# Merging the weights' sign into the exponent word on VectorE, with the prologue loads in one written list

## The chip, the cores and the metric

The kernel runs on one core of a Trainium2 chip. The metric is device time in microseconds (us) of one execution. Of the kernel before the change there are three timed runs: 801.87, 797.59 and 800.38 us, median 800.38 us. Every engine of the core has an instruction queue of its own, which it works through in order: TensorE (PE in the profile; its weight loads are PEld), VectorE (DVE), ScalarE (ACT), GpSimd (POOL) and SyncE (SP, which here only issues DMAs).

## The reference

Two stages. The first is a recurrence over 768 steps in 32 independent heads (batch 4, 8 heads of width 40). Its output is reshaped to 3072 tokens of width 320 and goes through a small network:

```python
for t in range(S):                       # state: (B, H, 40, 40)
    y[:, :, t] = einsum('bhd,bhde->bhe', rt, state)
    Sa = einsum('bhde,bhe->bhd', state, at)
    state = state * wt[:, :, None, :] - einsum('bhd,bhe->bhde', Sa, bt) + einsum('bhd,bhe->bhde', vt, kt)
h = x @ w_in                             # x: (3072, 320), w_in: (320, 2048)
out = (h * cos(h)) @ w_out               # w_out: (2048, 320)
```

The weights w_in and w_out arrive as float64, that is as pairs of 32-bit words, and the kernel turns them into float32 itself.

## The kernel before the change

The recurrence is cut into 24 chunks of 32 steps. For each chunk the kernel forms small triangular matrices and inverts them, and then carries the state on with a fixed series of steps: `ch_t` (transpose of the state), `ch_q`, `ch_x`, `ch_s` and `ch_z`, which leaves the new state in `qz` and the chunk's output in `yt`. In `ch_z` VectorE adds into `qz` (L755) and `yt` (L762), then GpSimd scales `qz` (L756) and `yt` (L767), and `tokens` sends `yt` through memory (`xd`) into the layout `xT` that the second stage reads. The loads of a chunk's k, v and r feed GpSimd's `p2_in` (copies to `vp` and `rp`, L586) and `p2_kn` (L593, L594). The network is worked on for two chunks at a time in pieces of four blocks of w_in and w_out (`first_a`, `first_b`, `second`); from chunk 2 on these pieces are dealt out between the recurrence's steps.

**The weights.** w_in and w_out are turned into float32 in 20 pieces of 128x512 (`rounded`), in this order of instructions per piece n:

- `fetch` (token `wf`): SP loads the words into a buffer that five pieces in turn share (from piece 7 on three).
- `taken` (`wt`): VectorE takes the mantissa bits (L245) and the exponent bits (L246) of the high word; ScalarE makes the float32 exponent (L249, Relu) and, in the kernel before, the sign of the high word as bf16 (L251).
- `mantissa` (`wm`): VectorE adds the low word to the mantissa (L255), ScalarE scales it (L258).
- `product` (`wp`): VectorE multiplies mantissa and exponent (L261); in the kernel before GpSimd then multiplies the result by the sign in place (L264).

The pieces are staggered. In program order one slot is `wm n`, `wt n+1`, `wp n`, then the fetch that takes over the buffer of piece n, and then the next slot. The slots lie between the recurrence's steps of chunks 0 to 3, from 48 to 140 us of the span. A fetch waits until the buffer's last reader is done, and everything behind it on SP's queue waits too.

**Idle matmuls.** In the same stage PE is given matmuls on zeros, whose results nobody reads: `busy` (128x512) and `spare` (128x192), in fixed numbers between the steps.

**What sets the order.** Inside `manual_schedule` each engine takes its instructions in the order in which they are written. In the kernel before that order comes out of a program of counters: `step` (L346) runs one step and then what is due after it (`later`, L343, so many steps later), and deals out the waiting parts of the weights and of the inverse. Instructions outside of `manual_schedule` (constants, the first loads of L182 to L201, and `warm`, L204, a Sin on one element that is there to load ScalarE's function table) are put into the queues by the framework's own scheduler.

Of the kernel before, what the change touches and what calls it, by code (L numbers as in the profile page):

```python
# [14 lines left out]


# [4 lines left out]
def kernel(  # L21
# [49 lines left out]
    NF = DFF // P  # L71
    N72 = C + D
# [109 lines left out]
    for c in range(2):  # L182
        load(c, "w", parts=range(2))
        load(c, "w", nc.scalar, range(2, 4))
    load(0, "a")
    load(1, "a", nc.scalar)
    for n, c in (("w", 2), ("w", 3), ("a", 2), ("a", 3), ("b", 2)):
        load(c, n)
    ws_fetch(1)
    load(3, "b")  # L190

# [8 lines left out]
    for c in range(2):  # L200
        load(c, "b", nc.gpsimd)  # L201
# [22 lines left out]
    def rounded(m, dst, src, by, by_sb):  # L224
# [3 lines left out]
        pool, tag = (  # L228
            ((sb2, "gT"), (sb2, "gT"), (sb1, "nt"), (sb1, "u"), (sb1, "inv"))[m % 5]
            if m < 10 else ((sb1, "nt"), (sb1, "u"), (sb1, "inv"))[(m - 10) % 3]  # L230
        )
# [9 lines left out]
        def taken():  # L241
            hi = t["words"][:, :, 1]
            t["mant"] = sb2.tile([P, WID], I32, tag="mant", name="mant")
            t["expo"] = sb2.tile([P, WID], I32, tag="expo", name="expo")
            nc.vector.tensor_scalar(t["mant"], hi, 0xFFFFF, None, ALU.bitwise_and)  # L245
            nc.vector.tensor_scalar(  # L246
                t["expo"], hi, 20, 0x7FF, ALU.logical_shift_right, ALU.bitwise_and
            )
            nc.scalar.activation(t["expo"], t["expo"], ACTF.Relu, bias=to_bits, scale=2.0**23)  # L249
            t["sign"] = sb2.tile([P, WID], mybir.dt.bfloat16, tag="sign", name="sign")  # L250
            nc.scalar.activation(t["sign"], hi, ACTF.Sign)  # L251
# [8 lines left out]
        def product():  # L260
            nc.vector.tensor_tensor(  # L261
                dst, t["mant"].bitcast(F32), t["expo"].bitcast(F32), ALU.mult
            )
            nc.gpsimd.tensor_tensor(dst, dst, t["sign"], ALU.mult)  # L264

        return fetch, taken, mantissa, product

    def weights():
# [5 lines left out]
        def put(dst, src, by, by_sb):  # L274
# [9 lines left out]
            work.append((fetch, none, none, lambda: nc.scalar.mul(dst, dst, by)))  # L284
# [52 lines left out]
    G = {"rest": []}  # L337

    waiting = []

    inv_steps, w_steps = [], []

    def later(steps, work):  # L343
        waiting.append([steps, work])

    def step(work, of_inv=0, of_w=0, small=False):  # L346


        before = list(waiting)
        work()  # L350
        G["small"] = small and G["kind"]
        for w in before:
            w[0] -= 1
            if w[0] == 0:
                waiting.remove(w)
                w[1]()
        for steps, n in ((inv_steps, of_inv), (w_steps, of_w)):
            for _ in range(min(n, len(steps))):
                steps.pop(0)()


    def p1_w(c):
# [21 lines left out]
        if c == 8:  # L384
            later(2, lambda: over_w(c, unpad(nat["w", c])))
        elif c >= 4:
            over_w(c, unpad(nat["w", c]))
# [18 lines left out]
    def p1_a(c):  # L406
        if c >= 4:
# [5 lines left out]
            over_w(c + 1, unpad(nat["w", c + 1]))  # L413
# [13 lines left out]
    def p1_b(c):  # L427
# [7 lines left out]
        if c == 2:  # L435
            G.pop("lower")()

    def p1_n(c):
# [15 lines left out]
        if c % 4 == 0:  # L454
            G["nt"] = sb1.tile([P, C, 4, 2, HH], F32, tag="nt", name="nt")
            if c < 8:
                G["noff"] = sb2.tile([P, 4, 2, HH, C], F32, tag="rt", name="noff")
        for e in range(2):
            nc.scalar.copy(
                G["nt"][:, :, c % 4 : c % 4 + 2, e, :].rearrange("p t c j -> p c j t"),  # L460
# [3 lines left out]
        def lower():  # L464
            for e in range(2):
                nc.scalar.copy(
                    G["noff"][:, c % 4 : c % 4 + 2, e, :, :].rearrange("p c j t -> p c (j t)"),
# [3 lines left out]
        if c == 0:  # L471
            G["lower"] = lower
        elif c < 8:
            lower()
        if c % 4 == 2 and c > 2:
            inv_space()

    def inv_space():
        G["inv"] = sb1.tile([P, C * C], F32, tag="inv", name="inv")
        nc.gpsimd.memset(G["inv"], 0.0)  # L480
        nc.gpsimd.memset(G["inv"][:, :: C + 1], -1.0)

    def inv_start():

        G["u"] = sb1.tile([P, C, C], F32, tag="u", name="u")
        nc.vector.transpose(
            G["u"].rearrange("p t s -> p (t s)"), G["nt"].rearrange("p t c e j -> p (t c e j)")
        )

    def inv_step(j):  # L490
        u, x = G["u"], G["inv"].rearrange("p (t s) -> p t s", t=C)
# [8 lines left out]
    def inv_end(c, part=False):  # L500
        rt = sb2.tile([P, 4, H, C], F32, tag="rt", name="rt")
        nc.vector.transpose(
            rt.rearrange("p c h t -> p t (c h)"), G["inv"].rearrange("p (t s) -> p t s", t=C)
        )
        G["rts"] = rt
# [8 lines left out]
    def pair_step(j):  # L514
        u, x = G["u"], G["inv"]
# [11 lines left out]
    def pair_turn(c):  # L527
        if c:
            G["rn"] = sb1.tile([P, 4 * H, HB], F32, tag="nt", name="rn")
            G["half"] = sb1.tile([P, 4 * H, C], F32, tag="u", name="half")  # L530
            nc.gpsimd.memset(G["half"][:, :, HB:], 0.0)
        else:
            G["rn"] = bn_b[6].rearrange("p h d -> p (h d)").rearrange("p (n u) -> p n u", u=HB)
        nc.vector.transpose(
            G["rn"].rearrange("p n u -> p u n"), pick(G["inv"], 0, (1, HB), (C, C)),
# [7 lines left out]
    def pair_half(c, i):  # L543
        return G["half"][:, H * i : H * (i + 1)] if c else bn_b[4 + i % 2][:, :, :C]

    def pair_first(c, i, moe=True):
        ps = pair_space(c, moe, ps_h, "h")
        nt = G["noff"].rearrange("p c e j t -> p (c e j) t")
        half = pair_half(c, i)
        for n in range(H):  # L550
            for g in range(B):
                mm(
                    ps[blk[g], HB * n : HB * (n + 1)], nt[blk[g], H * i + n, :],
                    G["rn"][blk[g], H * i + n, :], n == 0,
# [5 lines left out]
    def pair_second(c, i, moe=True):  # L560
        ps = pair_space(c, moe, ps_o, "o")
        half, rt = pair_half(c, i), G["rts"][:, i]
# [9 lines left out]
    def by_blocks(c):  # L572
        return [
            inv_start, *(lambda j=j: pair_step(j) for j in range(HB - 1, 0, -1)),
            lambda: pair_turn(c), lambda: inv_end(c, True),
        ]

    def inverse(c):
        return [
            inv_start, *(lambda j=j: inv_step(j) for j in range(C - 1, 0, -1)), lambda: inv_end(c)  # L580
        ]


    def p2_in(c):
        for dst, m in ((vp, "v"), (rp, "r")):
            nc.gpsimd.tensor_copy(  # L586
# [3 lines left out]
        landed(c)  # L590

    def p2_kn(c):
        nc.gpsimd.tensor_tensor(unpad(kn_b[c % 2]), nat["k", c], G["rw", c], ALU.mult)  # L593
        nc.gpsimd.tensor_copy(vvm[c % 2][:, :, C : C + D], nat["v", c])  # L594
        landed(c)

    def landed(c):

        G["users", c] = G.get(("users", c), 0) + 1
        if G["users", c] == 2 and c + 1 < NCH:  # L600
            for i, n in enumerate("kvr"):
                later(3 + i if c > 1 else 1, lambda n=n: load(c + 1, n))

    def p2_v(c):
# [3 lines left out]
        G["vT"] = sb3.tile([P, 4, P], F32, tag="opT", name="vT")  # L608
        G["rT", c] = sb2.tile([P, 4, P], F32, tag="rT", name="rT")
        nc.scalar.copy(G["vT"].rearrange("p j t -> p (j t)"), ps[:, 0])  # L610
        nc.scalar.copy(G["rT", c].rearrange("p j t -> p (j t)"), ps[:, 1])

    def p2_k(c):
        ps = at("kT")
        turned(ps[:, 0], kn_b[c % 2])
        G["kT"] = sb3.tile([P, 4, P], F32, tag="opT", name="kT")
        nc.scalar.copy(G["kT"].rearrange("p j t -> p (j t)"), ps[:, 0])

    def p2_g(c):
        kT, vT, aT, rT = G["kT"], G["vT"], G["aT", c], G["rT", c]  # L620
# [29 lines left out]
    def ch_t(c):  # L650
        ps = at("sT")
        n = DP + D
        G["s"] = sb1.tile([P, 2 * B, n], F32, tag="s", name="s")
# [4 lines left out]
        for i in range(2):  # L658
            nc.scalar.copy(G["s"][:n, 4 * i : 4 * i + 4].rearrange("p i e -> p (i e)"), ps[:n, i, : 4 * n])  # L659

    def ch_q(c):
        ps = at("qps")
        for i in range(2 * B):
            for e in range(2):
                for f in range(2):
                    mm(
                        ps[half[e], f, i * C : (i + 1) * C], G["s"][half[f], i, half[e]],
# [8 lines left out]
    def ch_x(c):  # L676
# [21 lines left out]
        G["x0"] = x0  # L698

    def ch_s(c):  # L700
        ps = at("sps")
        x0 = G["x0"]
# [21 lines left out]
        G["sm"] = sm  # L724

    def ch_z(c):
        ps = [at("dps") for _ in range(2)]
        sm = G["sm"]
# [41 lines left out]
        later(2, lambda: tokens(c, yt))  # L770

    def tokens(c, yt):

        xd = dram.tile([DM, P], F32, tag="xd", name="xd")
# [5 lines left out]
        if c % 2 == 0:  # L780
            G["xT"] = sb2.tile([P, 3, 2 * P], F32, tag="xT", name="xT")
        xT, toks = G["xT"], slice((c % 2) * P, (c % 2 + 1) * P)
        G["xT", c // 2] = xT
# [6 lines left out]
        later(1, back)  # L790


    def first_a(g, j):
        rest(3)
        G["ph"] = [ps_h.tile([P, 512], F32, tag="h", name="ph").rearrange("p (f t) -> p f t", f=2)
                   for _ in range(2)]
        G["gT", j] = sb2.tile([P, 4, 2 * P], F32, tag="gT", name="gT")
        first_full(g, j, 0)

    def first_full(g, j, e, fresh=True):  # L800
        xT, ph = G["xT", g], G["ph"][e]
# [5 lines left out]
    def first_b(g, j):  # L807
        xT, phs = G["xT", g], G["ph"]

        def tails(fresh):  # L810
            for f in range(2):
                for e in range(2):
                    for to in (full if G["small"] == "q" else [every]):
# [12 lines left out]

        us = [ph.rearrange("p f t -> p (f t)") for ph in phs]
        ns = [sb2.tile([P, 4 * P], F32, tag="turns", name="turns") for _ in range(2)]
        for u, n in zip(us, ns):
            nc.scalar.activation(n, u, ACTF.Identity, bias=rnd, scale=1.0)  # L830
        for u, n in zip(us, ns):
            nc.vector.scalar_tensor_tensor(n, n, -ROUND, u, ALU.add, ALU.subtract)  # L832
        gT = G["gT", j]

        def cosine(n):
            nc.scalar.activation(n, n, ACTF.Abs)  # L836
            nc.scalar.activation(n, n, ACTF.Sin, bias=half_pi, scale=-2.0 * math.pi)  # L837

        def product(e):
            nc.vector.tensor_tensor(  # L840
                gT[:, 2 * e : 2 * e + 2].rearrange("p f t -> p (f t)"), us[e], ns[e], ALU.mult
# [331 lines left out]
```

## Time and profile before

| | |
|---|---|
| timed runs | 801.87, 797.59, 800.38 us (median 800.38) |
| profiled execution, span from first to last instruction | 798.9 us |
| PE busy | 745.9 us (93%) |
| DVE busy | 486.7 us (61%) |
| ACT busy | 383.4 us (48%) |
| POOL busy | 199.9 us (25%) |
| L251, ScalarE's sign | 20 instructions, 13.3 us |
| L264, GpSimd's sign product | 20 instructions, 26.6 us |

The span of the profiled execution is the only time that is known of it; it lies inside the range of the three timed runs. The first 100 us differ from the rest: PE is not full there (17.10 us busy of 20 from 60 to 80 us, 15.65 from 80 to 100), and its granted clock is 0.82 to 0.92 in the 20 us slices up to 100 us and 1.00 in all later ones. From 320 us on PE is busy for 79.67 of 80 us and 390.00 of 398. The profile's lists name the source line, the engine, the operation and the tiles written and read; a start time is counted from the span's start, and "idle before" tells how long the engine had nothing to run and what ended that.

### The profile page before, as it was taken

What the parts mean: (1) busy time and instruction counts of PE and PEld (TensorE: products, weight loads), DVE (VectorE), ACT (ScalarE), POOL (GpSimd) and SP (SyncE); (2) the same over time, 40 slices, a digit from 0 to 9 for tenths busy, and PEclk for the clock granted to TensorE, in tenths of its full rate; (3) what the DMA queues carried; (4) which work ended last, traced back from release to release, by engine and by line L of the source; (5) the groups of instructions that cost most, each with busy time, mean ns of one, the idle gap of its engine ahead of it and who ended that gap; (6) DMA issues with size and microseconds to landing.
All of it is one profiled execution on the core that took longest, in us unless ns stands there. A gap on an engine that the chain in (4) does not pass through costs nothing.

```text
span 798.9 us, 39602 instructions
## 1 busy us (share of the span) xinstructions
PE 745.9 (93%) x17812; PEld 571.0 (71%) x17812; DVE 486.7 (61%) x1025; ACT 383.4 (48%) x723; POOL 199.9 (25%) x354
## 2 busy tenths in 40 slices
PE   4768798999999999999999999999999999999997
PEld 4535576777766777777777787777787777777775
DVE  8768858864734896554895645994346863323331
ACT  1336567564435436545535635534545445354352
POOL 5326635230321330330330230332031122201000
PEclk9888899999999999999999999999999999999999
DMA  8575563343353314334214324223220222001000
GB/s 112 150 187 140 146 152 88 60 124 64 59 122 64 67 36 65 72 99 70 60 38 66 93 43 73 46 49 68 43 46 21 46 46 55 19 18 32 20 17 16
DMA packets 183304, 55.79 MB, mean 70 GB/s; under 512 B 157152, under 2 KB 178656, under 8 KB 183136
## 3 DMA queue, kind: packets, MB, share of 16 engines
q1 hardware_dynamic: 177440, 52.11, 30.6%
q8 instruction: 140, 2.29, 1.2%
q10 hardware_dynamic: 5440, 0.82, 0.8%
q0 software_dynamic: 256, 0.33, 0.3%
q14 instruction: 28, 0.23, 0.1%
HBM read 42.07 MB, written 11.14 MB: 67 GB/s over the span
## 4 chain that ended last, share of the span: by engine, by line
PE 65%; DVE 14%; DMA 5%; ACT 5%; issue 4%; POOL 3%; SPq 2%; DVEq 0%; ACTq 0%; POOLq 0%
PE ph L101 22%; PE po L101 20%; PE x0ps L101 3%; PE dps L101 3%; PE gram L101 3%; DVE rw L395 3%; PE vT L330 2%; PE sps L101 2%; PE qps L101 2%; PE nps L101 2%; DVE inv_tmp L494 2%; DVE inv L498 2%; DVE mant L245 1%; SPq L152 1%; PE kT L330 1%
## 5 line engine op out<-in xcount | busy, mean ns | idle before, releaser
L101 PE MATMUL po<-w_out_sb,gT 128*128 128x320 f32 x768 | 223.5, 439 | 0.1
L101 PE MATMUL ph<-xT,w_in_sb 128*128 128x256 f32 x768 | 185.7, 386 | 0.1
L101 PEld LDWEIGHTS po<-w_out_sb,gT 128*128 128x128 f32 x768 | 140.2, 190 | 54.6 <-issue 2.3
L101 PEld LDWEIGHTS ph<-xT,w_in_sb 128*128 128x128 f32 x768 | 139.3, 190 | 29.7 <-issue 12.4
L830 ACT ACTIVATE turns<-ph,rnd 128x512 f32<-128x512 f32 x96 | 64.1, 685 | 156.3 <-PE ph L101 155.9
L832 DVE SCALAR_TENSOR_TENSOR turns<-turns,ph 128x512 f32<-128x512 f32 x96 | 64.0, 683 | 109.4 <-ACT turns L830 109.2
L840 DVE TENSOR_TENSOR gT<-ph,turns 128x512 f32<-128x512 f32 x96 | 65.8, 686 | 38.4 <-ACT turns L837 38.4
L756 POOL TENSOR_TENSOR qz<-qz,wc 128x160 f32<-128x160 f32 x92 | 41.9, 475 | 168.5 <-DVE qz L755 167.9
L837 ACT ACTIVATE turns<-turns,half_pi 128x512 f32<-128x512 f32 x96 | 69.3, 722 | 3.1
L836 ACT ACTIVATE turns<-turns 128x512 f32<-128x512 f32 x96 | 60.1, 626 | 19.0 <-DVE turns L832 19.0
L101 PE MATMUL ph<-xT,w_in_tail 64*128 64x256 f32 (+1 forms) x512 | 54.6, 394 | 1.6 <-issue 1.6
L498 DVE TENSOR_TENSOR inv<-inv,inv_tmp 128x31 f32<-128x31 f32 (+15 forms) x124 | 51.2, 413 | 4.3
L755 DVE TENSOR_TENSOR qz<-dps,qz 128x160 f32<-128x160 f32 x92 | 28.9, 314 | 37.6 <-PE dps L101 37.3
L586 POOL COPY vp<-nat_v 128x320 f32<-128x320 f32 x24 | 11.7, 487 | 159.9 <-DMA nat_v<-in_v_dram 139.6
L494 DVE TENSOR_TENSOR inv_tmp<-u,inv 128x31 f32<-128x31 f32 (+15 forms) x124 | 48.5, 391 | 2.3
L395 DVE RECIPROCAL rw<-nat_w 128x320 f32<-128x320 f32 x20 | 42.8, 2142 | 0.1
L101 PEld LDWEIGHTS ph<-xT,w_in_tail 64*128 64x128 f32 (+1 forms) x512 | 32.2, 160 | 10.8 <-issue 7.3
L767 POOL TENSOR_TENSOR yt<-yt,wb 128x512 f32<-128x512 f32 x24 | 31.6, 1318 | 22.1 <-DVE yt L762 22.1
L659 ACT COPY s<-sT 104x416 f32<-104x416 f32 x46 | 20.8, 503 | 33.1 <-PE sT L655 33.1
L719 DVE TENSOR_TENSOR sm<-sps,su 128x128 f32<-128x128 f32 x48 | 11.7, 285 | 33.1 <-ACT sm L714 30.3
L396 POOL TENSOR_TENSOR bn<-nat_b,rw 128x320 f32<-128x320 f32 x22 | 19.9, 905 | 44.3 <-DVE rw L395 44.2
L671 ACT COPY qz<-qps 40x512 f32<-40x512 f32 x46 | 26.6, 579 | 6.8 <-PE qps L101 6.4
(136 smaller groups left out, 1100.3 us busy)
## 6 DMA issues: line engine op xcount, KB each, us to landing
words<-in_moe_w_in_dram SPq DMA_DIRECT2D x8, 512.0 KB
xd<-yt SPq DMA_DIRECT2D x48, 80.0 KB
out_dram<-ot SPq DMA_DIRECT2D x24, 160.0 KB
nat_k<-in_k_dram SPq DMA_DIRECT2D x92, 40.0 KB
nat_v<-in_v_dram SPq DMA_DIRECT2D x92, 40.0 KB
nat_r<-in_r_dram SPq DMA_DIRECT2D x92, 40.0 KB
nat_a<-in_a_dram SPq DMA_DIRECT2D x84, 40.0 KB
ws<-in_w_dram SPq DMA_DIRECT2D x5, 640.0 KB
```

Source lines behind the costliest of these rows:

```text
L101: nc.tensor.matmul(o, lhsT=lhsT, rhs=rhs, start=start, stop=stop, skip_group_check=True)
L395: nc.vector.reciprocal(rw, wn)
L494: nc.vector.tensor_tensor(tmp, u[:, j : j + 1, :j].to_broadcast([P, C - j, j]), x[:, j:, j : j + 1].to_broadcast([P, C - j, j]), ALU.mult,)
L498: nc.vector.tensor_tensor(x[:, j:, :j], x[:, j:, :j], tmp, ALU.subtract)
L755: nc.vector.tensor_tensor(z, pick(dp, 0, (2 * N72 + C, 2), (N72, 2), (1, D)), z, ALU.add)
L756: nc.gpsimd.tensor_tensor(z, z, wc.rearrange("p (f m b) -> p f m b", f=2, m=2)[:, :, :, bb] .unsqueeze(3).to_broadcast([P, 2, 2, D]), ALU. ...
L767: nc.gpsimd.tensor_tensor(yt.rearrange("p j b t -> p (j b) t"), yt.rearrange("p j b t -> p (j b) t"), wx, ALU.mult)
L830: nc.scalar.activation(n, u, ACTF.Identity, bias=rnd, scale=1.0)
L832: nc.vector.scalar_tensor_tensor(n, n, -ROUND, u, ALU.add, ALU.subtract)
L836: nc.scalar.activation(n, n, ACTF.Abs)
L837: nc.scalar.activation(n, n, ACTF.Sin, bias=half_pi, scale=-2.0 * math.pi)
L840: nc.vector.tensor_tensor(gT[:, 2 * e : 2 * e + 2].rearrange("p f t -> p (f t)"), us[e], ns[e], ALU.mult)
```

## The change

**The sign.** ScalarE's Sign (L251) and GpSimd's product (L264) are gone. A new step `signed` (token `wg`), one VectorE scalar_tensor_tensor, takes the sign bit of the high word and merges it by bitwise or into the exponent word that ScalarE has made. It stands right ahead of `wp n`, so a slot becomes `wm n`, `wt n+1`, `wg n`, `wp n`, fetch. Since it reads the words once more, the buffer of piece n comes free after `wg n` and no longer after `wm n`.

```diff
             nc.scalar.activation(t["expo"], t["expo"], ACTF.Relu, bias=to_bits, scale=2.0**23)
-            t["sign"] = sb2.tile([P, WID], mybir.dt.bfloat16, tag="sign", name="sign")
-            nc.scalar.activation(t["sign"], hi, ACTF.Sign)
+
+        def signed():
+            nc.vector.scalar_tensor_tensor(
+                t["expo"], t["words"][:, :, 1], -(2**31), t["expo"], ALU.bitwise_and, ALU.bitwise_or
+            )
...
             nc.vector.tensor_tensor(
                 dst, t["mant"].bitcast(F32), t["expo"].bitcast(F32), ALU.mult
             )
-            nc.gpsimd.tensor_tensor(dst, dst, t["sign"], ALU.mult)
-
-        return fetch, taken, mantissa, product
+
+        return fetch, taken, mantissa, product, signed
```

**The written list.** The counters (`step`, `later`, `piece` and the rest of the control program) are replaced by a list of some 1,200 tokens, `PLAN`, which is read from left to right; each token calls one function (`do`). Its first part:

```python
L:0:w:s:l L:0:w:a:r L:1:w:s:l L:1:w:a:r L:0:a:s:x L:1:a:a:x L:0:b:p:x L:1:b:p:x pw:0 L:2:w:s:x L:3:w:s:x
L:2:a:s:x la:0:vr pa:0 L:3:a:s:x L:2:b:s:x sf:1 L:3:b:s:x wf:0 pw:2 la:0:k wf:1 pa:2 pb:0 pn:0 pb:2 lo:0 pn:2
...
B:5 ip:0:2 ip:0:1 k:1 B:2 it:0 ih:0 g:1 B:3 F:0:0:0 wt:0 wt:1 wf:3 wf:4 S:0:0:0 wm:0 wg:0 wp:0 s:0 wf:5 wm:1
wt:2 wg:1 wp:1 B:6 z:0 in:2 wf:6 wm:2 B:4 t:1 sf:2 kn:2 ld:4:a wt:3 wg:2 wp:2 wf:7 wm:3 B:3 F:0:1:0 tk:0 v:2
ld:4:w tb:0 wt:4 wg:3 wp:3 wf:8 wm:4 B:4 q:1 ld:3:k wt:5 wg:4 wp:4 wf:9 wm:5 B:5 k:2 ld:5:w ld:3:v wt:6 wg:5
wp:5 wm:6 wt:7 B:4 S:0:1:0 ld:3:r K:6 x:1 wg:6 wp:6 wm:7 wt:8 wg:7 wp:7 B:3 g:2 wf:10 wm:8 wt:9 wg:8 wp:8 B:3
s:1 in:3 wf:11 wm:9 wt:10 wg:9 wp:9 B:6 K:14 z:1 wf:12 wm:10 wt:11 wg:10 wp:10 B:4 K:6 t:2 kn:3 wf:13 wm:11
```

(`L` is one of the first loads with its chunk, tensor and queue, s for SP, a for ACT and p for POOL; `ld`, `la` and `sf` are other loads; `B` and `K` the idle matmuls; `in` and `kn` the GpSimd steps of a chunk; `tk` and `tb` the two halves of `tokens`.) Read out step by step, the counters of the kernel before give the same list, but for three things: the `wg` tokens; the first loads, which stood outside of `manual_schedule` and now stand in it, with the loads of a and b for chunks 2 and 3 written between the first steps; and one step without work that stood behind `fa:10:2`, so that in that piece `first_b` now starts with its wide matmuls and not with its narrow ones.

```diff
-    for c in range(2):
-        load(c, "w", parts=range(2))
-        load(c, "w", nc.scalar, range(2, 4))
-    load(0, "a")
-    load(1, "a", nc.scalar)
-    for n, c in (("w", 2), ("w", 3), ("a", 2), ("a", 3), ("b", 2)):
-        load(c, n)
-    ws_fetch(1)
-    load(3, "b")
...
     su = kept("su", [P, HH, C], 1, 1.0)[0]
...
-    for c in range(2):
-        load(c, "b", nc.gpsimd)
     half_pi = kept("half_pi", [P, 1], 1, math.pi / 2)[0]
     warm = kept("warm", [P, 1])[0]
     nc.scalar.activation(warm, half_pi, ACTF.Sin)
```

On SP the loads keep their order. On POOL the eight loads of b for chunks 0 and 1 now come behind the constants' memsets, where they came between `su` and `half_pi`. On ACT `warm` waits for `half_pi` alone, as before, which is now ready without those eight loads ahead of it. The buffers' rotation is the same (`WORDS`), the idle matmuls write to the newest output tile (`spare`) and not always to the first, and `product` of the network names its operands in two dimensions instead of one.

## The prediction

> **What bounds the kernel now.** I read the busy time by stretches first, then the chain of waits that ended last, then each engine in order of time from 47 to 145 us, the only stretch in which the two lines of the sign run.
>
> ```profile
> 60.00:80.00 20.00, 17.10 (x542) 10.39 (x530) 18.06 (x30) 13.67 (x24) 12.66 (x13) 0.87 0.55 139
> 80.00:100.00 20.00, 15.65 (x393) 10.28 (x392) 18.00 (x34) 12.10 (x23) 13.08 (x15) 0.87 0.55 146
> 100.00:120.00 20.00, 19.92 (x602) 15.81 (x601) 11.70 (x25) 13.33 (x25) 6.65 (x7) 1.00 0.67 153
> ```
>
> The columns behind the length are PE, PEld, DVE, ACT and POOL busy, the granted clock, and DMA. From 60 to 100 us VectorE is the full engine (36.06 of 40 us) and PE is not, although it is given idle matmuls; from 100 us on PE is. So the change can move the end through two doors: VectorE's queue between 62 and 91 us, and afterwards whatever PE waits for. The chain of waits says the same; it runs through the weights' own instructions:
>
> ```profile
> 80.43 0.60 DVE mant L255
> 81.03 1.30 DVE mant L245
> ...
> 86.75 0.64 ACT sign L251
> 87.40 0.38 ACT sm L714 x2
> 87.79 0.49 DVE sm L719 x2
> ...
> 90.70 0.87 POOL w_out_sb L264
> 91.81 0.61 POOL qz L756 x2
> ```
>
> Start, duration, what. Both removed lines stand on it: ScalarE's sign holds up the recurrence's `sm`, and GpSimd's sign product holds up the new state `qz`. PE sees it here:
>
> ```profile
> 88.43 0.32 PE L101 MATMUL dps<-idle 32*64 32x288 bf16 x4 [3.30 <-DVE sm L719]
> ```
>
> **The added instruction.** The nearest row is L255, the same kind on the same words: 20 times, 622 to 1352 ns, median 682, and 0.60 us from one start to the next (72.52, 73.12). Bounds: 0.34 us, the step from L246 to L245 (48.55, 48.89), one source; 1.35 us, L255 at 65.92 beside GpSimd's L593. I take 0.60, since it has L255's two sources: 20 x 0.60 = 12.0 us of VectorE.
>
> **What the removed product gives VectorE.**
>
> ```profile
> 80.58 1.47 POOL L264 TENSOR_TENSOR w_in_sb<-w_in_sb,sign 128x512 f32<-128x512 f32 x1 [3.50 <-DVE w_in_sb L261]
> 80.95 1.38 DVE L245 TENSOR_SCALAR mant<-words 128x512 int32<-128x512 int32 x1
> 85.27 0.42 DVE L245 TENSOR_SCALAR mant<-words 128x512 int32<-128x512 int32 x1
> ```
>
> Beside L264 L245 takes 1.38 us, alone 0.42: 0.96 us lost. In VectorE's order of time this happens beside L264 at 67.78 (L246), 70.29, 73.12, 75.97, 80.95 and 132.95 (0.96 each), 96.77 (0.83), 129.67 (L255, 0.59), 101.13 (0.23) and 119.36 (0.10): 7.5 us. So VectorE's work grows by 12.0 - 7.5 = 4.5 us. The Trainium skill (SBUF — State Buffer, section SBUF: two separate sides) says why: VectorE and GpSimd share one pair of ports, which whoever starts first holds for a whole instruction. It also speaks against the change, because an instruction of VectorE with two sources in SBUF is held by a GpSimd instruction that reads SBUF, and the added one is such; by it the slots beside what is left on GpSimd (L756, L767, L593) would pay again. The trace agrees with both, by the rows above and by the 1.35 us of L255.
>
> **47 to 62 us: nothing.** `wg 0` and `wg 1` fall into waits of VectorE: 1.24 us ahead of L261 at 52.27 (for ScalarE's L258) and 3.89 us before 60.45 (for PE). Without these covers it would be 1.2 us.
>
> **62 to 91 us: -3.3 us, before SP.** Between the two `ch_z` lie `wg 2` to `wg 9`, 8 x 0.60 = 4.8 us, and five of the delays, 5 x 0.96 = 4.8 us: VectorE's work stays level. What goes are its waits for ScalarE, 1.49 us ahead of L697, 0.73 ahead of L643 and 0.89 ahead of L719. Each is behind an exponent that came late because L245 was late, and behind a sign (78.41, 83.39, 86.75; 0.55 us each to the next start). I set the slots again one after the other: slot 2 keeps its delays beside L756 to L594, the next take 2.48 us (0.60 + 0.34 + 0.34 + 0.60 + 0.60) for 2.85. Then `wp 5` ends at 74.1 (before 75.37), L697 starts at 76.65 (79.38), `wp 7` ends at 80.7 (83.19) and `sm` starts at 84.45 (87.79), 3.3 us earlier. PE could take no more than 3.86: its idle matmuls end at 84.25, then it waited 0.56 and 3.30 us.
>
> **A wait that is added on SP.** `wf 7` was free after `wm 2` (issued at 63.21); now it waits for `wg 2`, behind both instructions of `wt 3` (63.07 to 65.06), until 65.7. Behind it on SP are `xd`, `nat_w`, `xT`, two more fetches and the loads of k, v and r of chunk 3, all nearly without a gap to 84.6. `xd` waited until 64.30 anyway, so they move by 1.9 us. Their reader is L586 at 88.08 (v) and 88.47 (r), which stands ahead of `qz` on POOL. r's last load was issued at 84.2; the chain has 2.21 us for the landing of such a load (k, at 15.26), so r was there at 86.4 and will be at 88.3, copied (0.45) by 88.7. `qz` starts then, against 91.81: -3.1 us, which is what the stage yields. This wait is what is late next; the 0.73 us that L264 held up `qz` (91.08 to 91.81) is inside this number. The fetches later on wait for their `wg` less than SP is behind.
>
> **91 to 145 us: +0.3 us.** `wg 10` to `wg 13` fall beside VectorE's 2.86 us wait at 106.42. In 107 to 121 us the sign's 0.55 us on ScalarE and the 0.60 us of `wg` nearly cancel, but `wg 15` stands ahead of L567, for which PE waited 0.72 us at 121.06: up to +0.6. In 122 to 140 us three `wg` cost 1.8 and give back 0.59 + 0.96; ScalarE's copies for PE (0.45 us wait at 133.82, 0.67 at 137.06) come up to 0.55 earlier: -0.6 to +0.3. **After 145 us** nothing has changed and PE is full, so the shift stays.
>
> **The prologue: -0.2 us.** On POOL the eight loads of b, 4.77 us from 2.74, move behind 2.4 us of memsets; they land at 11.2 now and are read by L396 at 12.83 and 15.43, so 2.4 us are nearly covered. `warm` comes earlier on ACT and with it the one table load that is needed, so that of 1.28 us at 6.40 goes; VectorE works without a gap from 8.04 to 15.9, but the chain does not pass there: L396 at 26.68 waits for b of chunk 3 (issued at 21.74, 4.78 us), at the end of SP's row of loads, 3 us after VectorE was ready. SP's order is the same. Bounds: -0.5 (a's loads without b's beside them) and +2 (ACT's loads of w held behind `warm` until 2.8 us instead of 0.81).
>
> **The rest.** `product` in two dimensions: L401 with sixteen short rows takes 669 ns, L840 686, so nothing. The other order of one `first_b`: under 0.2 us. The idle matmuls' other tile: no wait.
>
> **Sum.** -0.2 + 0 - 3.1 + 0.3 = -3.0 us. The profiled span of 798.9 becomes 795.9. The runs' median, 800.38, is 1.5 us above that span, so I predict 797.4 us. One thing I can't price well is PE's clock. After a wait the idle matmuls run slowly, 1.46 us for three at 90.64 against 0.81 at 94.43. If the 3.30 us wait goes, up to 1.6 us more is gained; if PE instead waits for `qz` at 89 us, as much is lost a little later. By the Trainium skill (TensorE: Matmul & The Clock Gate, section Part 1: The HAM clock gate) the clock is either half or full, decided over windows of about 3.4 us; the rows at 90.64 and 94.43 fit that, but do not tell where the window falls.
>
> **Rivals.**
> 1. *More is gained: 794.1 us.* The wait at 88.43 and the slow clock after it both go, r of chunk 3 isn't late because waits between the loads (one of v's issues takes 1.55 us) take up SP's 1.9 us, and ScalarE's relief counts at 133.82 and 137.06: -3.0 - 1.6 - 1.2 - 0.5 = -6.3. For it: POOL and ACT have gaps all through the stage. Against: PE is full from 100 to 120 us.
> 2. *Hidden anyway: 800 us.* PE's idle matmuls have fixed numbers; if they or PE's waits for "issue" (1.54 us at 78.50, 1.57 at 124.11) pace the stage, nothing is gained. Against: the 3.30 us wait.
> 3. *SP is late: 801.4 us.* Should the fetches fall further behind, `in 3` holds `qz` back. It turns to a loss once r lands more than 5.0 us later than 86.4 (86.4 + 5.0 + 0.45 is 91.8); at 6 us it costs 1.0 us.
> 4. *VectorE becomes the bound, slower: 804.9 us.* The place is the slots between `ch_z` 0 and 2. If ScalarE's waits are refilled, and GpSimd's remaining work blocks the new instruction as it blocked L255, VectorE's 4.5 us more count in full. It decides from the point at which VectorE has no idle time left; it has 3.94 us of 40 from 60 to 100 us. For it: that is little. Against: these waits are for ScalarE, which loses 13.3 us of work.
> 5. *The change doesn't do what it says:* the loads in the prologue come into another order (their numbered semaphores are handed out in turn), and ACT's queue stands still behind a large load: +2 to +5 on 797.4, 799 to 802.
>
> **How the numbers follow.** Chances: forecast 0.47 (795 to 799), rival 1 0.20, rival 2 0.11, rival 3 0.05, rival 4 0.10, rival 5 0.07. The bound of 0.5% is 4.0 us (796.4 and 804.4), about what a measurement of this kernel can tell from no change, as its three runs spread over 4.3 us. Faster: rival 1 and a third of the forecast, 0.36. Slower: rival 4 and a little of 3 and 5, 0.12. Same: 0.52. The range takes in the middles of all rivals and all bounds above: 792.5 to 805.0.
>
> **What would show it.** After the change L245 at 0.42 us in nearly all slots; L697 of chunk 1 before 77.5 us and PE's wait for `sm` under 1 us; `qz` of chunk 1 at about 88.7 us, right behind `rp`; `wf 7` at 65.7 us; L396's last load landing near 26.5 us; from 145 us on the same intervals. The prediction is wrong if VectorE shows long rows of L255's kind beside POOL, if `qz` starts after 91 us, or if the first 47 us are longer by more than 1 us.

## The result

The changed kernel is slower. In nine runs each, the kernel before took 797.59 to 803.40 us (median 800.42) and the changed kernel 801.69 to 809.74 us (median 806.44). The recorded ratio is 1.0059, with a 95% interval of 1.0034 to 1.0083; the two medians alone would give 1.0075. The median lies above the forecast's range (792.5 to 805.0). The profiled execution of the changed kernel is one of its shorter ones, 802.93 us with a span of 801.2 us; against the 798.9 us of before it shows 2.3 us of the loss, not all of it. VectorE's busy time went from 486.7 to 491.7 us, GpSimd's from 199.9 to 174.5, ScalarE's from 383.4 to 370.8.

Line numbers after the change: L318 and L319 are `taken` (before L245, L246), L325 is the new instruction, L331 the mantissa, L337 the product, L747 `sm`, L783 and L790 the additions into `qz` and `yt`, L615 `rt`, L310 the fetch of words on SP, L805 `xd`. First the busy time by stretches:

```profile
60.00:80.00 20.00, 14.94 (x539) 9.31 (x518) 18.31 (x36) 10.76 (x19) 6.73 (x9) 0.95 0.59 150
80.00:100.00 20.00, 16.98 (x399) 11.20 (x393) 16.85 (x37) 8.39 (x17) 7.27 (x9) 0.79 0.52 145
100.00:120.00 20.00, 19.53 (x600) 15.18 (x598) 12.79 (x25) 11.48 (x21) 1.16 (x3) 1.00 0.54 133
```

The columns are the stretch and its length, PE, PEld, DVE, ACT and POOL busy, the granted clock, the DMA share and GB/s. GpSimd is relieved (14.00 us from 60 to 100 instead of 25.74), and yet VectorE is as busy as before (35.16 us instead of 36.06). The chain of waits between 84 and 104 us tells what holds it:

```profile
85.17 4.13 DMA words<-in_moe_w_in_dram
...
89.39 0.43 DVE mant L318
...
91.47 0.32 DVE qz L783
...
95.88 1.29 DVE expo L325
...
97.19 0.33 SPq L310
...
98.04 0.37 SPq L805
...
98.45 2.88 DMA xd<-yt
```

The sign of ScalarE, `sm` and GpSimd's product, which stood on it before, are gone. In their place stand the words of piece 10, which SP could fetch only at 85.17, then the new instruction, then SP's queue behind it (fetch 13, and `xd` of chunk 1 behind that fetch). PE shows both sides:

```profile
86.31 0.76 PE L184 MATMUL dps<-idle 32*64 32x288 bf16 x8
...
91.97 0.59 PE L184 MATMUL busy<-idle 128*128 128x512 bf16 x1 [2.82 <-issue]
```

The wait of 3.30 us for `sm` went, as forecast (no bracket in the first line). But PE then had 2.82 us in which it waited for nothing that the profile shows, where it had 0.2 us before; and VectorE, in order of time, did this:

```profile
86.53 0.68 DVE L331 SCALAR_TENSOR_TENSOR mant<-words,mant 128x512 f32<-128x512 uint32 x1
89.39 0.43 DVE L318 TENSOR_SCALAR mant<-words 128x512 int32<-128x512 int32 x1 [2.19 <-DMA words<-in_moe_w_in_dram]
```

In the kernel before, the same two places of VectorE's queue, `wt 10` and the first addition into `qz`, have no wait:

```profile
89.00 0.67 DVE L245 TENSOR_SCALAR mant<-words 128x512 int32<-128x512 int32 x1
...
90.76 0.32 DVE L755 TENSOR_TENSOR qz<-dps,qz 128x160 f32<-128x160 f32 x1
```

PE's sums for chunk 1 were done at 88.4, but VectorE's queue stood at `wt 10`, for its words, with the additions into `qz` behind it. So `qz` started at 91.47; before it was 90.76.

### The profile page after: what moved, and what is told of

Its sections match the earlier page's. It is cut to its first block, busy times and chain, and to the rows that moved or that the text cites. A ratio compares the mean times of both kernels' runs of the same rounds, so it can differ in the third digit from the quotient of the medians.

```text
span 801.2 us, 39559 instructions
## 1 busy us (share of the span) xinstructions
PE 748.2 (93%) x17812; PEld 573.3 (72%) x17812; DVE 491.7 (61%) x1045; ACT 370.8 (46%) x702; POOL 174.5 (22%) x334
## 4 chain that ended last, share of the span: by engine, by line
PE 62%; DVE 14%; DMA 8%; SPq 5%; ACT 4%; issue 4%; POOL 2%; DVEq 0%; POOLq 0%; ACTq 0%
PE ph L184 21%; PE po L184 19%; SPq L235 4%; PE x0ps L184 3%; PE dps L184 3%; DVE rw L451 3%; PE gram L184 2%; PE vT L405 2%; PE sps L184 2%; DVE inv_tmp L542 2%; DVE inv L546 2%; DMA xd<-yt 2%; PE qps L184 2%; PE nps L184 1%; DMA xT<-xd 1%
## 5 line engine op out<-in xcount | busy, mean ns | idle before, releaser
L783 DVE TENSOR_TENSOR qz<-dps,qz 128x160 f32<-128x160 f32 x92 | 29.1, 316 | 35.3 <-PE dps L184 35.1
L747 DVE TENSOR_TENSOR sm<-sps,su 128x128 f32<-128x128 f32 x48 | 11.7, 285 | 31.3 <-ACT sm L742 28.5
L184 PEld LDWEIGHTS <-idle 128*128 128x128 bf16 (+2 forms) x268 | 18.2, 99 | 16.7 <-issue 10.2
```

What stands on the lines that cost most here:

```text
L184: nc.tensor.matmul(o, lhsT=lhsT, rhs=rhs, start=start, stop=stop, skip_group_check=True)
```

## The experiments

Each kernel was compared with runs of the kernel before on the same chip; ratios are to that kernel, with 95% intervals. "Old prologue" means the first loads as in the kernel before.

### The comparison itself

**c0_before**, no edit.

> The kernel before against itself, on the same chip as the next three: what the comparison gives for no change at all, and a profile on that chip. Expected by everyone: ratio 1.000, within 0.002.

Measured: 1.0014 (0.9991 to 1.0036). Differences of 0.15% mean nothing here. Start times of two profiles differ too: `qz` of chunk 0 starts at 60.45 us in the profile of the kernel before, at 61.80 in this one of the same kernel, and at 57.83 in e18_before_order, whose order of instructions is the same up to there. So a later start time is compared only where `qz` of chunk 0 agrees, or is counted from that `qz`.

### The two halves of the change

**e1_old_sign**, the prologue alone:

```diff
+            nc.scalar.activation(t["sign"], hi, ACTF.Sign)        # in taken
-            nc.vector.scalar_tensor_tensor(t["expo"], ...)         # in signed
+            nc.gpsimd.tensor_tensor(dst, dst, t["sign"], ALU.mult) # in product
```

> The changed kernel with the sign as before: ScalarE's Sign pass and GpSimd's product by it are back, the VectorE instruction of L325 is gone; the list and the prologue's order of loads stay as changed. Only the prologue differs from the kernel before (and one pair of matmul groups near the end). Theory (the buffers of words are given back later, after the next piece's L318 and L319, and SP's queue, the words and the recurrence follow late): the loss goes with the sign's part, the prologue's +0.6 us is absorbed before 62 us, so 800 to 801.5 us, ratio to before 0.999 to 1.002. Rival 5 (the prologue's order carries it): about 805 to 806 us. Rival of the clock alone: anything between, without order.

Measured: 1.0042 (1.0026 to 1.0058). Not what the theory expected: the prologue costs something by itself. PE's transposes of the last b in the prologue, first in the kernel before (c0_before), then here:

```profile
26.93 1.11 PE L330 MATMUL bT<-ident,bn 128*128 128x128 f32 x4 [1.70 <-POOL bn L396]
```

```profile
28.64 1.12 PE L406 MATMUL bT<-ident,bn 128*128 128x128 f32 x4 [4.15 <-POOL bn L453]
```

The b of chunk 3 comes last and is 1.7 us later.

**e2_old_prologue**, the sign alone:

```diff
+    for c in range(2):        # the loads of before, ahead of su and half_pi
+        load(c, "w", parts=range(2))
...
-L:0:w:s:l L:0:w:a:r ... sf:1 L:3:b:s:x
```

> The changed kernel with the prologue's loads in the order of before; the sign on VectorE stays. Theory: nearly all of the loss stays, 804 to 806.5 us (ratio 1.005 to 1.008); the last load of the prologue lands near 26.5 us again and PE's first chunk is 0.6 us earlier, but wf 13 still starts near 97 us. Rival 5 (prologue): back to 800 us or, with the gain that was forecast for the sign, 797 us.

Measured: 1.0065 (1.0045 to 1.0085), as expected. The sign alone loses as much as the whole change. Its profile shows the gain and its loss side by side; VectorE's rows (L325 is here `taken`, L790 `qz`) and PE's:

```profile
84.08 0.68 DVE L338 SCALAR_TENSOR_TENSOR mant<-words,mant 128x512 f32<-128x512 uint32 x1
88.47 0.43 DVE L325 TENSOR_SCALAR mant<-words 128x512 int32<-128x512 int32 x1 [3.72 <-DMA words<-in_moe_w_in_dram]
...
90.55 0.32 DVE L790 TENSOR_TENSOR qz<-dps,qz 128x160 f32<-128x160 f32 x1
```

```profile
85.59 0.86 PE L179 MATMUL dps<-sm,bn 32*40 32x72 f32 x62
...
90.08 0.38 PE L179 MATMUL busy<-idle 128*128 128x512 bf16 x1 [2.88 <-issue]
```

PE's last sums end at 86.45, `qz` starts at 90.55. Counted from `qz` of chunk 0 (57.97 here, 60.45 in the profile of before) PE's sums are 1.8 us earlier than before and `qz` is 2.3 us later: the gain is there, and more than it is lost between the two.

### Late buffers, or VectorE's time?

**e3_wg_early**, `wg n` right behind `wm n`:

```diff
-wm:9 wt:10 wg:9 wp:9
+wm:9 wg:9 wt:10 wp:9      # for every piece
```

> The changed kernel with the signed instruction of each piece (wg n) moved right behind the instruction of its mantissa (wm n) on VectorE, ahead of the next piece's L318 and L319 (wt n+1): the same instructions, only the order on VectorE differs, so that the buffer of words comes free without waiting for the next piece's words. Theory: wf 7 starts about 1 us earlier (65 us), wf 13 about 2.5 us earlier (95 us), xd of chunk 1 right after yt, and the time falls to 800 to 803 us. Rival 4 (VectorE's added 12 us are the bound): no change, 805 to 807 us.

Measured: 1.0059 (1.0040 to 1.0078). Nothing came back, although the fetches did: fetch 13 starts 3.30 us behind `qz` of chunk 1 (5.72 in the changed kernel, 2.54 before), `xd` 4.42 us behind it (6.57, 4.83). That speaks against the theory.

**e6_late_release**, the kernel before with a small reader of the words:

```diff
+        def signed():
+            nc.vector.tensor_scalar(seen, t["words"][:, :8, 1], 0xFFFFF, None, ALU.bitwise_and)
```

> The kernel before with its old sign on ScalarE and GpSimd and its old prologue; added is one VectorE instruction per piece that reads 8 columns of the words into a tile that nobody reads, at the place where the changed kernel has the signed instruction (behind the next piece's L318 and L319). It costs VectorE about 0.1 us, 20 times, and holds the buffer of words until then, as the change does. Theory (late release of the buffers): most of the loss without the change's instruction, wf 13 starts 2 to 3 us later than before's 93.3, ratio to before 1.003 to 1.006. Rival 4 (VectorE's 12 us more): 1.000 to 1.002.

Measured: 1.0013 (0.9994 to 1.0032), no different from c0_before. Fetch 13 started at 92.40, 4.01 us behind `qz` of chunk 1, so it was held, but less than in the changed kernel, and it was done before `yt` was ready (94.06): `xd` had not to wait for it. The place of the release alone costs nothing measurable, and e3_wg_early shows that taking the late fetch away brings nothing back. So the theory of the late buffers falls as the main cause.

**e4_short_sign**, the new instruction over 8 of 512 columns (the other columns' sign is left out), with the new prologue:

```diff
-                t["expo"], t["words"][:, :, 1], -(2**31), t["expo"], ...
+                t["expo"][:, :8], t["words"][:, :8, 1], -(2**31), t["expo"][:, :8], ...
```

> The changed kernel with the signed instruction over 8 of 512 columns only (the sign of the other columns is left out): the wait on the words' buffer and the place in VectorE's order stay, the instruction's own time falls from 0.68 us to about 0.1, 20 times, so VectorE's busy time falls by some 11 us. Theory (the place of the release decides, behind the next piece's wait for its words): a part comes back, through 0.6 us less per piece on VectorE ahead of the recurrence, 802 to 805 us, and VectorE still waits about 2 us for the words at wt 10 and wt 14. Rival 4 (VectorE's own added time is the bound): 797 to 799 us.

Measured: 1.0036 (1.0011 to 1.0060), about as much as the prologue alone (e1_old_sign), though the interval overlaps that of the changed kernel.

**e8_short_old** is the same with the old prologue.

> The sign on VectorE with the old prologue (as e2_old_prologue), the signed instruction over 8 of 512 columns (the sign of the other columns is left out): what the change would give if its VectorE instruction cost 0.1 us instead of 0.68. ScalarE's Sign passes and GpSimd's products are gone as in the change, and the buffers are given back as late as in the change. Theory, as it stands after e6_late_release (late release alone did next to nothing, 1.0013): VectorE's queue is the bound where it has no gap, between 126 and 145 us above all, and the instruction's own time is the cost; so no loss here, ratio 0.997 to 1.002. Rival (it is the order of the list, the words and SP's queue): the loss stays, 1.004 to 1.007.

Measured: 1.0021 (0.9996 to 1.0046), just above the theory's range. VectorE waits 5.67 us for the words of piece 10 here, longer for this piece than in any other profile, and yet little is lost: the late words seem to take the gain away rather than to make the loss.

**e9_double**, the instruction twice per piece:

```diff
+            for _ in range(2):
                 nc.vector.scalar_tensor_tensor(t["expo"], t["words"][:, :, 1], -(2**31), t["expo"], ...)
```

> The sign on VectorE with the old prologue, the signed instruction done twice per piece (the second one changes nothing in the values): 13.6 us more of VectorE's time in the same places. Theory (VectorE's time is the cost): another 3 to 5 us, ratio to before 1.009 to 1.013, PE's waits at x(3)'s and sps' inputs about 2 us longer. Rival (VectorE hidden, SP and the words decide): 1.006 to 1.008 as e2_old_prologue.

Measured, in four runs: 1.0171 (1.0142 to 1.0200), more than the theory expected. The medians' differences to before are 1.9, 5.2 and 14.0 us (e8_short_old, e2_old_prologue, e9_double) for 20 x 0.16, 20 x 0.68 and 20 x 1.36 us of VectorE: 3.3 us for the first 10.4, then 8.8 for the next 13.6. The intervals of e8_short_old and e2_old_prologue just meet, that of e9_double is clear of both. So the instruction's own time is on the path, and of the next 13.6 us a larger part is than of the first 10.4. PE's waits in e9_double, 62 to 170 us (total, times, longest):

```profile
PE dps L179 <- DVE sm L755: 5.0, 2, 3.8
PE ph L179 <- DMA xT<-xd: 3.3, 1, 3.3
PE gram L179 <- issue: 2.6, 1, 2.6
```

The wait for `sm` is back, at 3.8 us: VectorE is what PE waits for.

### Where it counts

**e5_order**, two moves in the list of e2_old_prologue:

```diff
-wm:9 wt:10 wg:9 wp:9 B:6 K:14 z:1 wf:12 ... kn:3 wf:13 wm:11 B:3 F:0:2:0 tk:1 v:3 tb:1
+wm:9 B:6 K:14 z:1 wt:10 wg:9 wp:9 wf:12 ... kn:3 tk:1 tb:1 wf:13 wm:11 B:3 F:0:2:0 v:3
```

> The sign on VectorE with the old prologue (as e2_old_prologue), and two moves in the list between 84 and 100 us: on VectorE the three instructions of the next piece that wait for its words (wt 10, wg 9, wp 9) stand behind z(1)'s additions instead of ahead of them; on SP the store and the read back of chunk 1's yt (xd, xT) stand ahead of wf 13 instead of behind it. The same instructions, the same order on PE, ScalarE and GpSimd. Theory (the gain is there, but VectorE's queue stands at wt 10 for words that SP's queue brings late, and xT stands behind the late release at wf 13): z(1)'s qz starts right behind PE's part, 86 to 88 us instead of 90.6, xT starts 94 to 97 us instead of 100.4, fa(0,0) by 100 us instead of 103.4; the time falls by 2 to 4 us against e2_old_prologue, ratio to before 0.999 to 1.003. Rival 4 (VectorE's added time is the bound): no fall, 1.005 to 1.008.

Measured: 1.0031 (1.0014 to 1.0048), just above the theory's range.

```profile
86.17 0.33 DVE L790 TENSOR_TENSOR qz<-dps,qz 128x160 f32<-128x160 f32 x1 [1.23 <-PE dps L179]
```

`qz` starts 4.4 us earlier than in e2_old_prologue, right behind PE, and xT of chunk 1 is read back from 96.26 instead of 100.44 (`qz` of chunk 0 agrees, 57.91 and 57.97). But PE's wait "issue" at the idle matmuls stays (90.25, 3.37 us), so `ch_t` starts where it did (91.59 and 91.64).

**e7_pool_w**, eight loads moved from SP to GpSimd:

```diff
-ld:4:w ... ld:5:w
+lp:4:w ... lp:5:w          # load(c, n, nc.gpsimd)
```

> The sign on VectorE with the old prologue (as e2_old_prologue); the eight loads of chunk 4's and 5's w (some 0.5 us each on SP's queue between 65 and 79 us) are issued by GpSimd, which the change has freed. Theory (from 64 to 85 us SP issues without a pause, and word piece 10 stands at the end of that): wf 10 starts 2 to 4 us earlier than 84.1 us, VectorE's wait of 3.7 us at wt 10 shrinks to 0 to 2 us, z(1)'s qz starts 1.5 to 4 us earlier; the time falls by 1 to 2.5 us against e2_old_prologue, the late release at wf 13 keeping the rest. Rival (SP waits for buffers, its issuing isn't the limit): wf 10 and the time unchanged. Rival 4: unchanged.

Measured: 1.0034 (1.0010 to 1.0058). In the words' place all was as expected: fetch 10 at 81.59 instead of 84.13, and VectorE's rows

```profile
85.55 0.43 DVE L325 TENSOR_SCALAR mant<-words 128x512 int32<-128x512 int32 x1 [0.24 <-DMA words<-in_moe_w_in_dram]
...
87.63 0.32 DVE L790 TENSOR_TENSOR qz<-dps,qz 128x160 f32<-128x160 f32 x1
```

So from 64 to 85 us SP's issuing, some 0.49 us per load of w, sets when the words come. Both ways of getting `qz` out from behind the words bring the ratio from 1.0065 to about half, though both intervals still overlap that of e2_old_prologue.

**e14_short_first** and **e15_short_last**, the short instruction in a part of the pieces:

```diff
+            n = 8 if 0 <= m < 12 else WID      # e15_short_last: 12 <= m < 20
```

> The sign on VectorE with the old prologue; the signed instruction is cut to 8 of 512 columns for pieces 0 to 11 (their other columns' sign is left out) and whole for pieces 12 to 19, which run from 101 us on. Theory (the instruction counts where VectorE has no gap, from 108 to 145 us): most of the loss stays, ratio 1.004 to 1.006. Rival (it counts evenly in all 20 pieces): 12 of 20 parts of the instruction's cost go, 1.003 to 1.004. Rival (it counts where PE waited for VectorE before, 62 to 91 us): 1.001 to 1.003.

> The other half: cut to 8 columns for pieces 12 to 19, whole for pieces 0 to 11. Theory: most of the loss goes, ratio 1.001 to 1.004, and x(3) and sps(3) start within 1 us of the kernel before. Rival (evenly): 1.004 to 1.005. Rival (62 to 91 us): 1.005 to 1.007.

Measured: 1.0029 (1.0003 to 1.0054) and 1.0010 (0.9987 to 1.0034). Either cut takes back most; the second fits the theory, the first is below its range. Their intervals overlap, so no part of the 20 pieces is shown to be the one that counts.

**e17_mixed_order** and **e18_before_order**, the moves of e5_order with the old sign for pieces 12 to 19, or for all:

```diff
+            if m >= 12:                        # e18_before_order: for every piece
+                nc.scalar.activation(t["sign"], hi, ACTF.Sign)
```

> Old prologue, the two moves of e5_order; pieces 0 to 11 have the sign on VectorE, pieces 12 to 19 as before on ScalarE and GpSimd. Theory (VectorE's time counts from 101 us on, before that the sign's removal from GpSimd frees VectorE as much as it costs): ratio 0.996 to 1.000, better than the changed kernel and at least as good as the kernel before. Rival (the instruction counts everywhere): 1.001 to 1.004.

> The kernel before with the two moves of e5_order only; the sign as before for all pieces. If the moves alone give the gain: ratio 0.997 to 0.999. Theory (in the kernel before VectorE comes to wt 10 after its words have landed, 89.0 us, and wf 13 isn't late, so there is nothing to gain from the moves): 0.999 to 1.002.

Measured: 1.0034 (1.0016 to 1.0051) and 1.0017 (1.0000 to 1.0035). The moves gain nothing without the change, as expected. The idea that the first twelve pieces cost nothing is not borne out: a ratio of 1.000 at most was expected. What those pieces cost isn't shown either, since the two intervals overlap.

### The prologue

**e10_b3_first**, e1_old_sign with one load moved; **e13_after_b3** has the same move in the changed kernel, **e16_before_b3** in the kernel before, **e11_order_b3** in e5_order:

```diff
-sf:1 L:3:b:s:x
+L:3:b:s:x sf:1
```

> As e1_old_sign (the old sign, the new prologue), with the load of chunk 3's b issued ahead of the 640 KB fetch of w (ws) on SP instead of behind it. In e1_old_sign the last four transposes of the prologue waited for that load 1.7 us longer than in the kernel before on the same chip. Theory (the late b3 is the prologue's whole cost): PE's first nps of chunks 2 and 3 start by 28 us instead of 30.4, and the ratio falls from 1.0042 to 0.998 to 1.001. Rival (what e1_old_sign loses comes from later places, PE's granted clock and its waits for instructions): PE earlier at 30 us but the ratio stays at 1.002 to 1.005.

> The changed kernel with the load of chunk 3's b ahead of the fetch of ws in its prologue, nothing else. If the late b3 and the VectorE instruction both count in the changed kernel: 2 to 3.5 us less than the changed kernel, ratio to before 1.001 to 1.004. If the instruction alone decides once it is there (VectorE's queue holds the recurrence whatever the prologue does): 1.005 to 1.007.

> The kernel before with the load of chunk 3's b ahead of the fetch of ws, nothing else. If the last load of the prologue is on the path in the kernel before too: PE's nps of chunks 2 and 3 start 1 to 2 us earlier and the ratio is 0.996 to 0.999. If the 47 to 62 us stage hides it: 0.999 to 1.002.

> As e5_order (sign on VectorE, old prologue, z(1)'s additions ahead of wt 10, xd and xT of chunk 1 ahead of wf 13), with the load of chunk 3's b ahead of the fetch of ws in the old prologue. If the 1.5 us of the prologue carry through, ratio 0.998 to 1.002, otherwise as e5_order, 1.002 to 1.005.

Measured: e10_b3_first 1.0002 (0.9977 to 1.0026), PE's transposes at 25.04 instead of 28.64:

```profile
25.04 0.66 PE L402 MATMUL bT<-ident,bn 128*128 128x128 f32 x4 [0.70 <-POOL bn L449]
```

e13_after_b3 1.0058 (1.0034 to 1.0082), e16_before_b3 0.9999 (0.9972 to 1.0026), e11_order_b3 1.0026 (1.0002 to 1.0049). By these ratios the late b of chunk 3 is the prologue's cost where the sign is old. The profile of e1_old_sign doesn't show where it is paid: its `qz` of chunk 0 starts at 60.46, that of the kernel before at 60.45. And e16_before_b3 shows that an earlier b gains nothing; with the sign on VectorE the move gives nothing, and the two costs don't add up (1.0042 and 1.0065 alone, 1.0059 together). No kernel here beats the kernel before.

## Why the prediction was wrong

**The failed step** is "62 to 91 us", with the wait that the prediction put behind it: "This wait is what is late next". That PE's wait for `sm` goes was right. What is late next was looked for in SP's loads of v and r (`qz` "right behind `rp`", 88.7), and they were in time: r's loads went 0.4 us later than before, not 1.9, and `rp` was copied at 86.76. The words of piece 10 were missed. They are issued behind r on the same queue, and `wt 10`, which reads them, stands ahead of `qz` on VectorE. Before, VectorE came to `wt 10` at 89.00 without a wait; the words (issued at 84.74) had no need to be earlier. As soon as VectorE came earlier it waited: 2.19 us here, 3.72 in e2_old_prologue, 0.24 with SP relieved (e7_pool_w), and with the additions ahead of it `qz` started at 86.17 (e5_order). Forecast for the stage were -3.1 us at GpSimd's `qz`; it started at 91.87, before at 91.81, and VectorE's `qz` 0.7 us later than before. VectorE's own part was sized too large as well: `sm` was to come at 84.45 and came at 86.13 (before 87.79), half of the 3.3 us.

**The second step that failed is "91 to 145 us: +0.3".** From `qz` of chunk 1 to VectorE's copy of x(3) it was 54.19 us before and 56.20 after: +2.0. In this profile the lateness first runs over SP. The sentence "the fetches later on wait for their `wg` less than SP is behind" was wrong for fetch 13: it started at 97.19 instead of 93.30, held by `wg 10`, and `xd`, ready at 95.59, went at 98.04. The words of piece 14, further back on SP, then held VectorE 2.5 us later than before (first line before, second after):

```profile
107.64 0.43 DVE L245 TENSOR_SCALAR mant<-words 128x512 int32<-128x512 int32 x1 [0.76 <-DMA words<-in_moe_w_out_dram]
```

```profile
110.15 0.43 DVE L318 TENSOR_SCALAR mant<-words 128x512 int32<-128x512 int32 x1 [1.93 <-DMA words<-in_moe_w_out_dram]
```

From 122 us on VectorE itself has no gap worth naming, as these rows show:

```profile
122.03 0.42 DVE L318 TENSOR_SCALAR mant<-words 128x512 int32<-128x512 int32 x1
122.37 0.42 DVE L319 TENSOR_SCALAR expo<-words 128x512 int32<-128x512 int32 x1
122.70 0.68 DVE L325 SCALAR_TENSOR_TENSOR expo<-words,expo 128x512 int32<-128x512 int32 x1
123.42 0.69 DVE L337 TENSOR_TENSOR w_out_sb<-mant,expo 128x512 f32<-128x512 f32 x1
124.03 0.28 DVE L615 TENSOR_TENSOR rt<-rt,below 128x128 f32<-128x128 f32 x1
```

```profile
124.36 0.32 PE L184 MATMUL dps<-idle 32*64 32x288 bf16 x4 [1.78 <-DVE rt L615]
```

The step had seen that `wg 15` stands ahead of `rt`, and priced it at up to +0.6; PE waited 1.78 us for it, 0.72 before. At x(3) the kernel is 2.7 us late. Both ways begin at the new instruction; since e3_wg_early has no wait for the words of piece 14 and loses as much, the way over SP is not the cause alone.

**The instruction's price** was too low. From the start of L325 to that of L337 it is 0.71 to 0.79 us in 16 of 20 pieces (median 0.79), and 17.1 us for all 20, not 12.0. In e3_wg_early, where the next piece's `taken` follows it and not the product that reads its result, the next start is 0.60 to 0.61 us later wherever nothing else holds it (68.82 to 69.42, 84.22 to 84.83). Beside GpSimd it took 1.36 us (95.80, beside L628, `kn`), as the upper bound said, so the trace goes on agreeing with the Trainium skill's page SBUF — State Buffer (section SBUF: two separate sides). What the removed product gives back was right: L318 takes 0.41 to 0.43 us in 17 of 20 pieces, and VectorE's busy time grew by 5.0 us (forecast 4.5); the 0.1 us without work ahead of each product is not in it.

**The rivals.** Rival 4 (VectorE becomes the bound, 804.9) came nearest, in its price and in that VectorE's added time is what costs; e9_double with e8_short_old is the evidence. Its condition was wrong, though: it was to decide when VectorE has no idle time left, but from 62 to 91 us VectorE is still idle for 4.3 us of 29 (24.73 busy), 2.19 of them at `wt 10`. In that stage it is not VectorE's capacity that binds but the order in its queue. Rival 5 (loads in another order, +2 to +5) gave the price of the prologue taken alone, +4.2 us in e1_old_sign, but not by its mechanism: SP's order is the same, and the last load of b was only issued later (20.71, before 20.12). In the changed kernel it adds nothing that can be measured. Rival 3 (SP is late) had the right queue and the wrong load. Rival 2 (PE's waits for "issue" pace the stage) is in part true: in e5_order `qz` came 4.4 us earlier and `ch_t` did not. The forecast of -0.2 for the prologue had the wrong sign, its bound of +2 held (`bn` at 27.28 instead of 26.68).

**47 to 62 us** was right (`qz` of chunk 0 at 60.37, before 60.45), and so was fetch 7 (65.95, forecast 65.7). **"After 145 us nothing"** was not: at 172.76 PE waited 1.56 us for "issue" and its granted clock from 175 to 179 us was 0.73. That wait is in e1_old_sign as well (169.37) and in neither profile of the kernel before. Why it comes in some kernels, and how much of the 6.0 us between the medians it makes, stays open; the two profiles that are compared here differ by 2.3 us only, and are 2.7 us apart at x(3) already.

## What to carry to other kernels

When a wait goes, go through every instruction that stands ahead of the freed one in the same in-order queue, and ask of each when its data lands; here the next bound was a transfer that until then came just in time. Price an added instruction at the place where it stands (with what reads its result right behind it, and with what waits behind it), not by the engine's total. And in a row of loads, look at which one the first reader needs last before its neighbours are moved.

## What the runs showed of the hardware

PE's waits called "issue" come at the same places of its program in nearly every profile. From the one at 75.59 us (x0ps) to those at 79.60 (gram), 91.97 (idle matmuls) and 172.76 (gram) of the changed kernel the trace has 256, then 512, then 3584 instructions of PE (128, 255 and 1776 matmuls, as many weight loads or one more, and 0, 1 and 32 semaphore instructions), that is 1, 2 and 14 times 256. A packet of 16384 bytes of the queue that the page calls "instruction" landed 1.2 to 1.6 us before each of the four ended, for the one at 91.97 from 89.79 to 90.72. The Trainium skill (Runtime: NRT & Kernel Launch, section Instruction fetch mechanics) says that instructions come in blocks of 16 KiB, 256 instructions, and that fetching them is mostly hidden. The block agrees; the hiding does not hold for rows of short matmuls like these, where such a wait lasted up to 3.64 us (e11_order_b3, at 91.78). That these packets are what PE waits for is inferred, no run here varied them.

The granted clock in the trace is only ever full or half, in stretches of 3.41 us or multiples of it (the last one is cut by the trace's end). Eight such stretches of half speed lie in the first 100 us of the kernel before, thirteen in those of c0_before, the same program in another run.
